# Routed attention and a feed-forward block on one core: group maxima kept in PSUM, one load moved, and a new order of the first batch

## The chip, the cores and the metric

The kernel runs on one core of one Trainium2 chip. The metric is the device time of one execution in microseconds (us); the median of the runs counts. Engines are named as the profile names them: PE (TensorE), DVE (VectorE), ACT (ScalarE), POOL (GpSimd) and SP (the queue from which nearly all transfers are started).

## The reference, cut to what matters

```
q, k, v: 4 batches x 8 heads x 768 tokens x 64;  centroids: 8 heads x 16 x 64
q_assign = argmax(normalised q . normalised centroids)     # same for k
mask     = q_assign[i] == k_assign[j]
attn     = softmax(where(mask, q k^T / 8, -1e9))
x        = (attn v), heads side by side                    # 3072 x 512
h    = x @ w_in                                            # 3072 x 1024
solu = h * softmax(h)
ln   = (solu - mean) / sqrt(var + 1e-6) * g_ln
out  = ln @ w_out                                          # 3072 x 512
```

## The kernel before, in words

**The work.** Heads are taken in pairs, four pairs for each of four batches; a step of batch b, pair p, is called by its kind and b.p. For each pair, queries (i = 0) and keys (i = 1) are loaded (`ld`, L388 for the first batch and the next batch's first pair in two big loads, L419 in eight small ones afterwards), turned so that the 64 channels of two heads lie on partitions, and multiplied by the normalised centroids (`cl`: the cluster products, L469 or L474, into the PSUM tile `csc`). VectorE transposes the products out of PSUM (`tb`, L483), takes the largest of each group of 16 (`mx`, L496), compares each product with its group's largest (`oh`, the one-hot rows, L502 or L508) and transposes these back (`ot`, L518 or L521). The one-hot rows are then copied under the channels of q and k (`pl`, L536 to L551), beside the casts of q and k to bfloat16 (`ca`, L452 to L456). A score matmul over channels and one-hot rows together applies the mask: two tokens of one cluster get 256 more, which the exponential's bias takes off again.

**The first five pairs** (0.0 to 0.3 and 1.0) are "apart": TensorE turns the tokens (`tp`, L400, three transposes each) and VectorE or ACT copies them out of PSUM (`xa`, L407); in later pairs VectorE transposes them itself (`xt`, L425). The very first pair is worked on head by head, in steps with a further index, so that head 0 can start before head 1 has been loaded.

**Attention.** Scores come in banks of 128 keys x 512 (`S`, L637, three PSUM buffers), ACT takes the exponential (`E`, L643, nine SBUF buffers), TensorE multiplies by v with a column of ones (`V`, L660) and VectorE divides (`N`, L672 and L685) into x. v is loaded by `lv` (L563) and cast by `cv` (L568, POOL). In batch 0 the row blocks are ordered so that the first rows of all heads are done early.

**Feed-forward.** For each block of 128 rows x is transposed by a DMA on SP's queue (`tx`, L715), multiplied by w_in (`h`, L746), and VectorE takes the row maximum (`hm`, L752), ACT the exponential (`ex`), VectorE the product (`u`, L765) and its statistics (`bn`, `ag`), SP's queue the transpose of u (`tu`), TensorE the second product (`y`, L810), ACT or VectorE the scaling (`sc`), SP's queue the store (`ou`). The weights are loaded by `li` and `lo`, w_in is cast by `wi` (POOL, L587), g is transposed by `gt` (TensorE, L594), and w_out is centred by `su`, `sk`, `me` and eight steps `ce` (L623, VectorE). The second row block's first matmul (h1.0.0) needs the bank of PSUM from which the last `ce` reads.

**What sets the order.** `Weave.ORDER` (L28 to L84) is a written order for each of the engines SP, POOL, PE, DVE and ACT. A word such as `S2` stands for the next two steps of kind S; `=pl0.0.1.0.0` takes a step by its name. Each engine works strictly through its list; waits between engines follow from the data. Steps that share the PSUM buffer "m" (`cl`, `gt`, `y`) take it and hand it back (`take`, `give`): the cluster products hold it until `tb` has transposed them out (L1030). Before the list begins, the centroids, the first pair's queries and keys and its v are loaded (L841 to L845); `lv0.0` in SP's list is an empty step. `fl` are filler matmuls.

Of the kernel before, what the change touches and what calls it, by code (L numbers as in the profile page):

```python
# [10 lines left out]
F32 = mybir.dt.float32  # L11
# [11 lines left out]
class Weave:  # L23
# [6 lines left out]
        ld4 lv si ld2 lg ld2 lv ld2 lv li lo ld2 lo lv ld2 lo2 ld6 li3 tx lv ld tx ld7 lv tu ld5 lv  # L30
        tx tu ld2 ou ld tu ld10 lv ou tu ld6 tu lv ld lv ld6 ou ld tx ld tu ld3 ou2 ld tx ld3 lv ld
        tu ld tx ld tu ld8 ou ld6 ou ld tu ld3 pl ld3 ou lv tu lv tu ld2 ou ld2 ou tx ld tu tx lv
        ld3 =pl3.2.1.1 pl ou lv2 tx ou tu2 ou pl tu2 tx2 tu ou tx ou tu tx tu ou tx ou tu ou tu ou
        tu ou5
    """
    ORDER["POOL"] = """
        z po zo =ca0.0.0.1.0 cf pl =cv0.0.1 =ca0.0.1.1.1 ca cv =ca0.1.0.1 z =pl0.0.1.0.0
        =pl0.0.1.1.1 pl2 =z5 =ca0.1.1.0 =ca0.1.1.1 ca =ca0.2.0.1 =ca0.2.1.1 pl =pl0.1.0.0 pl2
        =ca0.2.1.0 ca =cv0.1.1 cv =ca0.3.0.1 cv pl =pl0.2.0.0 =pl0.2.0.1 pl gs cv =ca0.3.1.1
        =ca0.3.1.0 ca pl =pl0.3.0.0 sg pl z pl cv ca wi cv =pl1.0.0.1 pl cb pl2 wi =ca1.0.1.0 wi2  # L40
        =ca1.1.1.0 ca2 =cv1.0.1 cv ca =ca1.1.1.1 z at =pl1.1.0.1 pl at pl bl ca al pl =ca1.2.0.1 at
        =cv1.1.1 =ca1.2.1.1 cv =ca1.2.1.0 al ca al =pl1.2.1.1 =ca1.3.1.0 =pl1.2.0.0 pl cv bl pl cv2
        ca2 =pl1.3.1.1 ca pl2 at2 bl al pl =ca2.0.1.1 =ca2.0.1.0 ca =pl2.0.0.1 =pl2.0.1.1 pl2 at
# [143 lines left out]
def kernel(  # L187
# [15 lines left out]
    P = 128  # L203
# [1102 lines left out]
```

## Time and profile before

| what | value |
|---|---|
| median of three runs | 224.43 us (224.42 to 225.3) |
| the profiled execution, its own time | 224.15 us |
| its span from the first to the last instruction | 222.4 us |
| mean moved by the DMA engines | 38.80 MB, 174 GB/s |
| exponentials of the scores (L643) | 288, 150.3 us busy on ACT |
| score matmuls (L637) | 648, 98.4 us busy on PE |
| comparisons of the first five pairs (L502) | 6, 348 to 1717 ns |

The page of the profile gives the busy time of each engine, the chain of work that ended last (followed back from the last instruction to whatever released each step), and the groups of instructions by line. A row of a timeline or of the chain reads: start, duration, engine, line or tile, and how many instructions were merged; in square brackets stands the idle time of the engine just before it and what ended it. A merged row's duration runs from the first start to the last end, so single durations overlap a little with the next one. "To landing" is the time from the issue of a DMA to its completion.

### The profile page before, as it was taken

How to read it: one execution, taken by the hardware profiler on the slowest of the kernel's cores; microseconds unless marked ns; L12 is line 12 of the kernel's file. 1: busy time of each engine (PE TensorE's matmuls, PEld its weight loads, DVE VectorE, ACT ScalarE, POOL GpSimd, SP SyncE). 2: the span in 40 equal slices, each digit the busy share in tenths (PEclk: the TensorE clock that was granted, in tenths of full speed). 3: DMA queues.
4: the chain of work that ended last, by engine and by line, in shares of the span. 5: the costliest groups of instructions: out<-in, count | busy, mean ns of one | idle time of the engine just before them, and what ended most of it. 6: DMA issues, size and time to landing. Idle time of an engine off the chain costs nothing.

```text
span 222.4 us, 6659 instructions
## 1 busy us (share of the span) xinstructions
PE 213.6 (96%) x2437; PEld 144.4 (65%) x2470; DVE 194.9 (88%) x348; ACT 192.4 (87%) x370; POOL 132.9 (60%) x257
## 2 busy tenths in 40 slices
PE   7799999999999999999999999999999999999993
PEld 7587675676666677676567666776675776664442
DVE  2888698899999989988999999898999998889981
ACT  4699898999999999998998998988998999884362
POOL 4589969991684686475968856794448330125231
PEclk9999999999999999999999999999999999999999
DMA  6999998499999999799998969997953415858722
GB/s 197 362 381 352 221 114 266 92 184 175 181 179 144 200 152 235 145 151 211 203 159 156 197 108 255 191 159 169 274 85 84 71 27 124 135 121 115 218 93 96
DMA packets 117327, 38.80 MB, mean 174 GB/s; under 512 B 105640, under 2 KB 112816, under 8 KB 117296
## 3 DMA queue, kind: packets, MB, share of 16 engines
q1 hardware_dynamic: 116864, 37.87, 81.7%
q10 hardware_dynamic: 432, 0.52, 0.7%
q8 instruction: 19, 0.31, 0.6%
q14 instruction: 12, 0.10, 0.2%
HBM read 23.11 MB, written 6.29 MB: 132 GB/s over the span
## 4 chain that ended last, share of the span: by engine, by line
PE 84%; DVE 9%; DMA 2%; issue 1%; ACT 1%; SPq 0%; ACTq 0%; DVEq 0%
PE sps L637 27%; PE hreg L746 17%; PE yps L810 16%; PE ops L660 15%; PE csc L474 4%; PE hreg L400 3%; DMA raw<-in_k_dram 2%; DVE w_out_c L623 2%; DVE x L685 1%; PE csc L469 1%; DVE nmax L752 1%; PE hreg L609 1%; DVE u L765 1%; DVE bs L776 1%; PE hreg L810 1%
## 5 line engine op out<-in xcount | busy, mean ns | idle before, releaser
L643 ACT ACTIVATE e<-sps 128x512 bf16<-128x512 f32 x288 | 150.3, 606 | 10.4 <-PE sps L637 8.5
L637 PE MATMUL sps<-qk 80*128 80x256 bf16 (+3 forms) x648 | 98.4, 260 | 0.3
L637 PEld LDWEIGHTS <-qk 80*128 80x128 bf16 (+1 forms) x648 | 51.6, 97 | 34.0 <-issue 10.2
L660 PEld LDWEIGHTS <-e 128*128 128x128 bf16 x1152 | 52.7, 97 | 11.5 <-PE sps L637 1.1
L660 PE MATMUL ops<-v,e 128*128 128x65 bf16 x1152 | 57.7, 193 | 0.6 <-DVE x L685 0.5
L746 PE MATMUL hreg<-w_in_sb,xT 128*128 128x512 bf16 x175 | 50.4, 379 | 1.2 <-DMA xT<-x 0.2
L810 PE MATMUL yps<-w_out_c,uT 128*128 128x512 bf16 x168 | 46.8, 378 | 0.7
L765 DVE TENSOR_TENSOR u<-e_sb,hreg 128x1024 bf16<-128x1024 bf16 (+1 forms) x25 | 28.9, 1160 | 4.0 <-ACT e_sb L758 3.7
L550 POOL COPY qk<-oht 32x384 f32<-32x384 f32 x40 | 20.3, 507 | 19.3 <-DVE oht L521 14.5
L776 DVE BATCH_NORM_STATS2 bs<-u 128x6 f32<-128x512 bf16 x48 | 31.7, 674 | 0.1
L752 DVE TENSOR_REDUCE nmax<-hreg 128x1 f32<-128x1024 f32 x24 | 29.1, 1213 | 2.5 <-PE hreg L746 2.2
L758 ACT ACTIVATE e_sb<-hreg,nmax 128x1024 bf16<-128x1024 f32 x24 | 26.9, 1119 | 3.3 <-DVE nmax L752 3.2
L792 POOL TENSOR_SCALAR esq<-es,mv 128x1 f32<-128x1 f32 x24 | 8.5, 354 | 33.7 <-DVE mv L780 33.0
L454 POOL CAST qk<-xt 64x768 bf16<-64x768 f32 (+1 forms) x32 | 26.3, 823 | 2.6 <-ACT xt L407 0.8
L456 POOL TENSOR_SCALAR qk<-xt 64x768 bf16<-64x768 f32 (+1 forms) x29 | 24.3, 839 | 2.9 <-PE sps L637 1.2
L810 PEld LDWEIGHTS <-uT 128*128 128x128 bf16 x200 | 17.9, 97 | 10.8 <-issue 0.2
L746 PEld LDWEIGHTS <-xT 128*128 128x128 bf16 x192 | 16.6, 97 | 9.2 <-DVE u L765 1.0
L425 DVE STREAM_TRANSPOSE xt<-raw 128x768 f32<-128x768 f32 x22 | 20.7, 953 | 0.0
L685 DVE TENSOR_TENSOR x<-ops,den 128x256 bf16<-128x256 f32 (+1 forms) x39 | 19.0, 486 | 1.3
L568 POOL CAST v<-vf 128x384 bf16<-128x384 f32 x29 | 14.7, 514 | 3.2 <-PE sps L637 2.3
L825 ACT ACTIVATE y<-yps,alpha 128x512 f32<-128x512 f32 x13 | 8.9, 688 | 7.6 <-PE yps L810 5.8
L795 POOL TENSOR_TENSOR alpha<-esq,halves 128x1 f32<-128x1 f32 x24 | 13.4, 560 | 2.0
(87 smaller groups left out, 178.5 us busy)
## 6 DMA issues: line engine op xcount, KB each, us to landing
vf<-in_v_dram SPq DMA_DIRECT2D x16, 384.0 KB, 4.7
out_dram<-y SPq DMA_DIRECT2D x23, 256.0 KB, 2.7
raw<-in_q_dram SPq DMA_DIRECT2D x44, 96.0 KB, 3.7
raw<-in_k_dram SPq DMA_DIRECT2D x44, 96.0 KB, 3.6
w_st<-in_moe_w_in_dram SPq DMA_DIRECT2D x4, 512.0 KB, 6.7
w_g<-in_moe_w_out_dram SPq DMA_DIRECT2D x4, 512.0 KB, 9.3
raw<-in_q_dram SPq DMA_DIRECT2D x4, 384.0 KB, 7.1
raw<-in_k_dram SPq DMA_DIRECT2D x4, 384.0 KB, 7.5
```

The lines of the kernel that those rows point to most:

```text
L454: VEC[e].tensor_copy(dst, src)
L456: VEC[e].tensor_scalar(dst, src, scalar1=inv_C, scalar2=1.0, op0=Alu.mult, op1=Alu.mult)
L637: nc.tensor.matmul(sps_[n, k][:, c0:c0 + w], side(b, h // 2, 1, h % 2, keys)[r], side(b, h // 2, 0, h % 2, slice(s0 * P, s0 * P + w))[r])
L643: nc.scalar.activation(es[n, k][:, :w], sps_[n, k][:, :w], Act.Exp, scale=exp_scale, bias=-exp_scale)
L660: nc.tensor.matmul(opss[g][:, s, :VW], es[n, k][:, c0:c0 + P], v1[slot(b, h // 2)][:, h % 2, kt, :VW], start=(kt == 0), stop=(kt == n_t - 1))
L685: nc.vector.tensor_tensor(dst, src, dn, op=Alu.mult)
L746: uses(nc.tensor.matmul(hreg[:, at(f, f2)[1], :], xTs[f][:, dc, :], w_in_sb[:, dc, f2 * FF2:(f2 + 1) * FF2], start=(dc == 0), stop=(dc == ...
L752: uses(nc.vector.tensor_reduce(ff[f, "nmax"][:], pair_of(f), axis=AXY, op=Alu.max, negate=True), *both(f))
L758: uses(nc.scalar.activation(ff[f, "e"][:], pair_of(f), Act.Exp, bias=ff[f, "nmax"][:], accum_out=ff[f, "esum"][:]), *both(f))
L765: uses(nc.vector.tensor_tensor(ff[f, "u"][:, at_], ff[f, "e"][:, at_], pair_of(f)[:, at_], op=Alu.mult), *banks)
L776: nc.vector.bn_stats(ff[f, "bs"][:, f2, :], ff[f, "u"][:, f2, :])
L810: ins = nc.tensor.matmul(dst, ff[f, "uT"][:, at(f, f2)[0] * (n_fc // 2) + c, :], w_out_c[:, fc, cols], start=(fc == chunks[0]), stop=(fc = ...
```

## The change

1. **Maxima in PSUM.** For the pairs 0.1, 0.2, 0.3 and 1.0 the tile `csc` is made 24 columns wider, and `mx` writes the group maxima into these columns, where they were written to an SBUF tile before. `oh` reads them from there. The buffer "m" is therefore handed back after `oh` and not after `tb`. The first pair (two half steps) and all later pairs keep the SBUF tile.
2. **The first v.** Its load leaves the place right behind the first pair's queries and keys and becomes the step `lv0.0` of SP's list, behind both loads of pair 0.1 and the queries of pair 0.2.
3. **New orders** for the first batch and the beginning of the second, on all five engines; from `ld2.0.0.0` (SP), `al1` (POOL), `h3.1.0` (PE), `bn2.0` (DVE) and `E29.1` (ACT) on, the lists are as before. Which engine does which step is unchanged. Six of 22 filler matmuls are dropped. Among the moves: on ACT `xa0.0.0.1`, `ca0.0.0.0.0` and `ca0.0.1.1.0` come before `xa0.0.1.1`, `ca0.0.0.1.1` goes in front of the first exponential and `ca0.0.1.0.1` behind the fifth; on PE `tp0.1.0.0` goes in front of `cl0.0.1` and `tp0.1.0.1` in front of the first scores, `cl1.1` goes behind the first feed-forward block (`h0.0.0` to `h0.1.1`), which moves up; on POOL `cv0.0.0` goes behind `ca0.1.0.1` and `ca0.1.1.0`; on DVE `xa0.3.0.1` goes behind N0, `ot0.2` before `xa0.3.1.1`, `xt1.1.1` behind seven centrings, `tb1.1` and `mx1.1` behind the last one; on SP `li0` goes three loads back, `li1` to `li3` and `tx0` come in front of the last two loads of pair 1.1, and `lv1.0` behind most of pair 1.2.

The diff, its orders cut to the lines in question:

```diff
     ORDER["SP"] = """
-        ld4 lv si ld2 lg ld2 lv ld2 lv li lo ld2 lo lv ld2 lo2 ld6 li3 tx lv ld tx ld7 lv tu ld5 lv
+        ld4 si ld3 lv ld lg lv ld2 lv ld lo ld lo ld lo li ld lv lo li ld4 li2 tx ld9 lv ld tx ld tu
+        ld5 lv tu lv ld tx ld tu ou ld10 lv ou tu ld6 tu lv ld lv ld6 ou ld tx ld tu ld3 ou2 ld tx
...
     ORDER["POOL"] = """
-        z po zo =ca0.0.0.1.0 cf pl =cv0.0.1 =ca0.0.1.1.1 ca cv =ca0.1.0.1 z =pl0.0.1.0.0
-        =pl0.0.1.1.1 pl2 =z5 =ca0.1.1.0 =ca0.1.1.1 ca =ca0.2.0.1 =ca0.2.1.1 pl =pl0.1.0.0 pl2
-        =ca0.2.1.0 ca =cv0.1.1 cv =ca0.3.0.1 cv pl =pl0.2.0.0 =pl0.2.0.1 pl gs cv =ca0.3.1.1
-        =ca0.3.1.0 ca pl =pl0.3.0.0 sg pl z pl cv ca wi cv =pl1.0.0.1 pl cb pl2 wi =ca1.0.1.0 wi2
+        z po zo =ca0.0.0.1.0 ca cf pl ca =z4 =z3 =ca0.1.0.1 =ca0.1.1.0 sg cv =pl0.0.1.0.0
+        =pl0.0.1.0.1 =pl0.0.1.1.1 pl cv ca2 =pl0.1.0.0 =ca0.2.1.1 =pl0.1.0.1 pl cv2 pl ca =ca0.2.1.0
+        =pl0.2.0.1 =pl0.2.0.0 ca pl z =ca0.3.1.0 pl =cv0.2.1 ca =ca0.3.1.1 cv pl =pl0.3.0.0 gs ca
+        =cv0.3.1 =pl0.3.0.1 pl cv =pl1.0.1.1 pl3 wi cb wi =ca1.0.0.1 wi2 =ca1.0.1.0 z ca =ca1.1.0.0
...
     ORDER["PE"] = """
-        wm fl2 cp tp fl2 tp ci tp fl4 cl tp fl6 cl fl8 tp S2 tp S tp S tp S V tp V S3 cl S2 tp2 S2 tp S V
-        gt V3 tp S2 tp S cl S2 V tp V S V S tp S V2 S V S2 cl S V S2 tp V S V2 S2 tp S V2 S tp S V S
-        tp V S3 cl S2 V2 S V2 S2 su S V S V S V2 S2 su S2 V2 S2 V2 S2 me S2 V S V2 S2 V S cl S3 V3 S
-        V S h2 S3 h2 S2 V2 S V S V S h2 V S V S h S V2 S2 h S h S V S V S h S V S V S y2 V2 S y S h2
+        wm fl2 cp tp fl2 tp ci tp fl4 cl tp fl8 tp cl tp S3 tp3 S tp S2 cl S tp S2 V tp V2 S2 V gt S V
+        tp2 S2 V cl S V S tp S2 V S tp V S2 tp V S2 V2 S2 cl S V S V S V2 S2 tp S tp S V S V S tp V
+        S2 V S cl S3 V4 S2 su S V S2 V3 S2 su S3 V4 S3 me S V S2 V S V S V S2 V2 S2 h S V S h V S h
+        S h S V S V S V2 S cl S h2 S V S h S V S V S V h S3 V h V S V S V h S y2 S y V S2 h2 S3 y V
...
     ORDER["DVE"] = """
-        cn cg ca tb mx oh ot pl2 tb xa mx xa oh ot =xa0.1.1.1 xa2 tb mx oh xa gk ot xa N tb mx xa oh
-        xa ot N2 tb =xa1.0.0.1 xa mx xa2 N oh ot tb mx N oh ot N sk xt N xt ce2 N ce3 tb ce2 N mx hm
-        ce N u xt bn N hm oh ot bn xt u ag N bn hm sc bn u tb bn N bn mx hm oh =ag2 ag =xt1.3.1 ot u
+        cn cg ca tb mx oh ot pl2 xa tb xa3 mx oh ot xa tb mx oh xa gk ot N tb mx =xa0.3.1.0 xa oh ot
+        xa N tb mx oh N xa =xa1.0.1.0 xa2 ot N tb N mx oh ot N sk N xt ce3 N ce4 xt N hm ce N u bn
+        tb bn mx ag N hm =xt1.2.1 oh u ot bn xt hm sc N u tb bn2 N bn mx hm oh =ag2 ag =xt1.3.1 ot u
...
     ORDER["ACT"] = """
-        wa ct xa2 ca cj =xa0.0.1.1 xa =ca0.0.1.0.1 =ca0.0.1.1.0 pl E5 ca E5 xa E2 xa E xa E56 ex E12
-        ex E7 ex E11 ex sc E8 ex E3 ca E21 ex E17 sc E5 ex E3 sc E4 ex E9 ex E11 ex E5 sc E9 ex E13
+        wa ct xa3 cj ca =ca0.0.1.1.0 xa pl ca E5 ca E3 xa E4 xa2 E56 ex E11 ex E8 ex E12 ex sc E8 ex
+        E3 ca E21 ex E17 sc E5 ex E3 sc E4 ex E9 ex E11 ex E5 sc E9 ex E13 ex E20 ex E5 sc E2 ex E11
...
-        csc = ps_m.tile([P, HALF], F32, name="csc", tag="m")
+        csc = ps_m.tile([P, HALF + HALF // NC_], F32, name="csc", tag="m")
...
-        asg[b, p, hf, "mx"] = pr.tile([P, HALF // NC_], F32, name="mx")
+
+        asg[b, p, hf, "mx"] = (asg[b, p, hf, "csc"][:, HALF:] if apart(b, p) and hf is None else
+                               pr.tile([P, HALF // NC_], F32, name="mx"))
...
             load_head(0, 0, i, hh, nc.sync if i else nc.scalar)
-    load_v(0, 0)
...
-            add(f"lv{t}", "SP", 0.0, -1990, lambda e: None, [], last_ld[-1:], move=1.3)
+            add(f"lv{t}", "SP", 0.45, -990, (lambda e, b=b, p=p: load_v(b, p)), [], last_ld[-1:], move=1.05)
...
                 [f"cl{t}"] + ([f"oh{old}"] if old else []),
-                give="m")
+                give=None if apart(b, p) and not half else "m")
...
                 also={"POOL": 0.7},
+                give="m" if apart(b, p) and not half else None)
...
-                            ("si", "SP", 3.95)):
-        add(name, eng, busy, -1000, lambda e: None, [], ["lv0.0"] if eng == "SP" else [])
+                            ("si", "SP", 3.95)):
+        add(name, eng, busy, -1000, lambda e: None, [], ["ld0.0.1.1"] if eng == "SP" else [])
```

More of the change, by code (lines that the diff above doesn't have):

```diff
@@ new lines @@
+        V S V cl S2 V2 S y S2 y S V S V S V2 S y S2 y S V2 S2 V2 h S2 h2 S h S2 h S V y V2 S V y S
+        V2 y2 S2 h3 S V S2 V cl V h2 S2 V cl S V S V S h S2 h S y S h S V2 y2 S2 y V2 S2 h S V2 S2 h
+        S h2 V2 S V S2 V h y2 V S2 y S V y S2 h S2 V2 cl S V S h S V S2 cl S V2 S h2 S y S V S y V
+        S2 V y2 V h S V S h V S2 cl S2 V S y V y3 S V S V S y S2 V2 S V2 S y S2 y S y V3 S V S2 h2
+        S2 h2 V S V S V S y S V S y S y V S V h y S2 h S h2 S2 V3 S2 V h V cl S h S h S V S2 h S V S
@@ L1029 @@
                 (lambda e, b=b, p=p, hf=hf: turn_back(b, p, hf)),
-                [f"cl{t}"] + ([f"oh{old}"] if old else []), give="m")
+                [f"cl{t}"] + ([f"oh{old}"] if old else []),
+                give=None if apart(b, p) and not half else "m")
             add(f"mx{t}", "DVE", 0.37 if half else 0.56, first - 9,
@@ L1035 @@
                 [f"mx{t}"] + ["zo"] * apart(b, p) + [f"ot{x}" for x in last[-1:]] * (apart(b, p) and not half),
-                also={"POOL": 0.7})
+                also={"POOL": 0.7},
+                give="m" if apart(b, p) and not half else None)
             nd = [f"oh{t}"]
```

32 lines of the change are left out of this document (13 added, 19 removed).

## The prediction

> **What bounds the kernel now.** I read the span and the clock first, then the busy shares and the chain that ended last on the page, then that chain in order of time, then single engines in the stretches where the chain leaves TensorE.
>
> ```profile
> core 0: 222.4 us, clock 1.000
> ```
>
> ```profile
> PE 213.6 (96%) x2437; PEld 144.4 (65%) x2470; DVE 194.9 (88%) x348; ACT 192.4 (87%) x370; POOL 132.9 (60%) x257
> ...
> PE 84%; DVE 9%; DMA 2%; issue 1%; ACT 1%; SPq 0%; ACTq 0%; DVEq 0%
> ```
>
> The clock is full throughout, so nothing here is throttling. TensorE carries 84% of the chain. The change leaves the matmuls themselves alone (it drops six filler matmuls), so what can be won is the 16% in which the chain is elsewhere. It leaves TensorE for long in three places that the edited orders reach:
>
> ```profile
> 1.63 5.31 DMA raw<-in_k_dram
> 6.98 0.56 PE hreg L400 x3
> 7.56 0.86 ACT xt L407 x2
> 8.84 0.52 ACT qk L452
> 9.39 0.52 ACT qk L536
> 10.04 0.60 PE sps L637 x4
> ...
> 23.26 0.53 DVE xt L407
> 23.79 0.88 DVE w_out_c L518
> 24.79 0.57 DVE x L685
> ...
> 43.79 1.97 DVE w_out_c L623 x3
> 45.76 0.49 DVE cst L483
> 46.26 1.29 DVE w_out_c L623 x2
> 48.10 0.46 DVE mx L496
> 48.56 1.23 DVE nmax L752
> 49.79 0.67 DVE w_out_c L623
> 50.50 0.60 PE hreg L746 x2
> ```
>
> Place one, up to 10.04: the first scores (S0.0, head 0 of the first pair) wait for a copy of one-hot rows on ACT (9.39, L536). That copy stands in ACT's queue behind copies and casts of head 1, whose keys land at 1.63 + 5.31 = 6.94. Place two, 23.26 to 25.36: VectorE is late with a copy of turned tokens, a transpose of one-hot rows and the division N1. Place three, 43.79 to 50.46: VectorE works through the centring of w_out (L623) with other work strewn between, and the first matmul of the second feed-forward row block (50.50) waits for its last piece. The written orders of all engines run together again by about 65 us, so from there I take over the shift that has been reached.
>
> **The change, part by part.**
>
> *The start.* In the new ACT order only one copy of head 1 (xa0.0.1.1) stands between the landing and the one-hot copy: it ends at 7.56 + 0.43 (half of 0.86) = 7.99. The one-hot copy then waits for the transposed one-hot rows instead, which VectorE has ready when its own two copies of them begin:
>
> ```profile
> 8.58 0.57 DVE L536 COPY qk<-oht 16x192 f32<-16x192 f32 x2
> ...
> 21.61 1.72 DVE L502 TENSOR_TENSOR w_out_c<-cst,mx 128x384 bf16<-128x384 f32 x1
> ...
> 31.30 0.55 DVE L502 TENSOR_TENSOR w_out_c<-cst,mx 128x384 bf16<-128x384 f32 x1
> ...
> 43.15 0.18 DVE L672 RECIPROCAL den<-ops 128x4 f32<-128x4 f32 x1 [0.55 <-PE ops L660]
> ```
>
> VectorE's copies end at 9.15, ACT's at 8.58 + 0.52 = 9.10. TensorE now has three steps in front of S0.0: transposes of the second pair's queries (tp0.1.0.0), head 1's cluster products, more transposes (tp0.1.0.1).
>
> ```profile
> 8.47 0.53 PE L469 MATMUL csc<-xt,w_out_c 128*32 128x192 f32 x8 [0.62 <-ACT xt L407]
> ```
>
> The first needs its data. Today those queries are the second load behind head 1's keys (v is the first):
>
> ```profile
> 2.58 0.47 SPq L388 DMA_DIRECT2D raw<-in_q_dram  x1
> ```
>
> ```profile
> raw<-in_q_dram SPq DMA_DIRECT2D x1, 384.0 KB, 6.4
> ```
>
> They land at 2.58 + 6.4 = 8.98, which is 2.04 behind the keys, so 1.02 for each load of 384 KB. Without v they take the first slot, 7.96. Then the transposes end near 8.5 (0.56 for three), the products near 9.05, the second transposes near 9.4 when pipelined and at 9.6 when not. S0.0 starts near 9.35 instead of 10.04. ACT's cast ca0.0.0.1.1 moves in front of the first exponential (0.52 from 9.10 on) and fits beside S0.0; ca0.0.1.0.1 takes its old place behind the fifth. **Gain at the start 0.7 us**, between 0.4 (10.04 less 9.6) and 0.9 (less 9.15).
>
> *v three loads later* lands in the fourth slot, 6.94 + 4 x 1.02 = 11.0. Its cast on POOL now stands behind two casts of the second pair, the later of which needs VectorE's fourth copy of turned tokens: 9.15 + 4 x 0.53 + 0.49 (a transpose between) = 11.8. A cast of this size takes
>
> ```profile
> 18.15 0.83 POOL L456 TENSOR_SCALAR qk<-xt 64x768 bf16<-64x768 f32 x1
> ```
>
> so POOL reaches v near 12.6, 1.6 us after it has landed. Behind v on POOL are four one-hot copies that head 1's scores need. At no more than ACT's 0.52 for each of the five, they end by 15.2. The exponentials get to head 1 after nine of 0.52 (8.77 / 17, below), a cast and a copy: 9.8 + 4.7 + 0.95 = 15.4. Price nothing; past that cover each microsecond falls on ACT, one to one.
>
> *The maxima in PSUM.* For four pairs the maximum is written beside the products, and the comparison (L502) reads one operand from SBUF and one from PSUM. The same comparison took 1.72 at 21.61 and 0.55 at 31.30. I take 0.55 for all, the nearer row: 1.17 us less in VectorE's queue ahead of N1. The other end is that the 1.72 stays; no row shows a PSUM operand dearer, the division at 24.79 reads PSUM and takes 0.57. By the Trainium skill, SBUF — State Buffer, section Who interferes with whom, a VectorE operation with two SBUF inputs contends with a GpSimd operation that reads SBUF, and one with a single SBUF input does not; the trace agrees in that 0.55 and 1.72 are the same instruction on the same shapes. Another of its rules speaks against the change: Perfetto Trace Analysis, section Optimizing Scalar/DVE Operations, puts the overhead of a VectorE instruction at about 125 ns on PSUM and 60 on SBUF. By that, as an estimate, the eight edited instructions would cost 0.5 us more and the total gain would be 1.1 us; the row of 24.79 shows nothing of it.
>
> The price: the PSUM buffer comes free after the comparison, later by a maximum and a comparison (0.46 + 0.55 = 1.0). Next in it is the transpose of g on TensorE, behind that the scores S3.2 and all that follow; ACT waits for these. Three banks of scores in hand last 3 x 0.52 = 1.5 us, so I price it at nothing, at most 1.0 if they are used up.
>
> *Place two.* ACT shows what it costs:
>
> ```profile
> 25.10 0.60 ACT L643 ACTIVATE e<-sps 128x512 bf16<-128x512 f32 x1 [0.58 <-PE sps L637]
> 26.16 8.77 ACT L643 ACTIVATE e<-sps 128x512 bf16<-128x512 f32 x17 [0.46 <-PE sps L637]
> ```
>
> Behind it 17 exponentials run without a gap, so ACT's loss of 0.58 + 0.46 = 1.04 is real. N1 comes earlier by 1.17 (the comparison) and 0.7 (the start), near 22.9, and the copy that cluster products cl0.3 need stays in front of it. **Gain 1.0**, between 0 and 1.04. Sum so far 1.7.
>
> *Place three* is a queue of VectorE. The new order takes a transpose out of PSUM (0.49) and a maximum (0.46) from in front of the last centring. It puts a transpose of tokens (xt1.1.1; 0.9, like the one at 23.79) in, which so far stood ahead of all centrings. One centring (0.66, a third of 1.97) goes into the idle 0.55 at 43.15. Net gain 0.6, so the last centring ends 2.3 earlier, near 48.2. But the 0.95 comes back right behind it, on an engine that is 88% busy: 1.4 for VectorE at 65 us, 1.7 for TensorE. **I carry 1.6 on**, with 0.7 and 2.3 as ends.
>
> *SP's queue.* The last two of the eight loads for the second batch's second pair now stand behind the first transposing DMA of x (tx0), which waits for the division N6:
>
> ```profile
> 40.33 1.86 SPq L715 DMA_TRANSPOSE xT<-x  x1
> 42.30 0.52 SPq L563 DMA_DIRECT2D vf<-in_v_dram  x1
> 42.91 0.61 SPq L419 DMA_DIRECT2D raw<-in_q_dram  x1
> ```
>
> ```profile
> raw<-in_q_dram SPq DMA_DIRECT2D x1, 96.0 KB, 3.9
> ```
>
> With 1.7 gained it starts near 38.6 and ends near 40.5; the last load is issued 0.6 later and lands 3.9 after that, at 45.0. VectorE's xt1.1.1 wants it at 47.55 (where the sixth and seventh centrings end) less 1.7, 0.49 and 0.55: 44.8. Price 0.2, inside my rounding. The first feed-forward matmul is moved up too, closer behind the casts of its weights on POOL; 0 to 0.83, one cast, taken as 0.
>
> **Sum.** 0.7 + 1.0 = 1.7; place three's 0.6 is more than paid back by the 0.95 on VectorE, which leaves 1.4 there and 1.7 on TensorE: 1.6 us. The profiled execution took 224.15 (span 222.4); it becomes 222.55. The median of the runs shown is 0.28 above it, so 222.8 stands for the median. About 0.5%, 1.12 us, is what a measurement of this kernel can tell from no change: faster means below 223.3, slower above 225.55.
>
> **The rivals.**
>
> *Only the start is kept.* Place two comes back at another wait, or the comparison stays at 1.72. For it: TensorE is 96%, VectorE 88% and ACT 87% busy, so an engine that is freed soon meets another. Against: 17 exponentials in a row show no other stall of ACT for 9 us. Gain 0.7, time 223.7: same.
>
> *The last key load comes late.* The transpose xt1.1.1 waits, and behind it in VectorE's queue a division, the maximum of the first row block and the last centring; TensorE waits at the matmul of 50.50. Each microsecond beyond a landing of 3.9 counts one to one, and the 0.95 behind it can't be caught up. With VectorE's 1.4 it decides from a landing of 5.3 us; at 7.0, a little over the 6.4 that a load took in the full queue of the start, the kernel is 1.7 slower: 226.1. For it: a transposing DMA is right ahead in the queue. Against: the load issued at 42.91 had one ahead as well, and took 3.9.
>
> *More is won.* VectorE's idle time behind 50 us absorbs the 0.95, and 2.3 stays, or 2.5 with the start at its better end: near 222.0.
>
> **How the numbers follow.** Forecast 0.48, more won 0.10: faster, 0.58. Only the start 0.27: same. The late load 0.15: slower. The range takes in the better end with what lies between runs (221.4), the start-only case, and the late load up to a landing of 6 us, which is 0.7 slower (225.1). The forecast's own range is 222.2 to 223.5.
>
> **What would show it.** Right: first scores near 9.4; four comparisons near 0.55; no idle of ACT near 0.5 between 20 and 27; the gapless run of exponentials that began at 26.16 beginning near 24.5; the last centring ending near 48.2. Wrong: a comparison over 0.8; VectorE idle in front of xt1.1.1 with the load of keys as releaser; TensorE idle in front of the first L746.

## The result, and the profile after

The kernel after takes 226.2 us (median of 22 runs, 224.05 to 229.79), the kernel before took 224.43 us beside it (22 runs, 223.64 to 226.34). The ratio is 1.0056, 95% interval 1.0036 to 1.0075: slower by 1.3 us, where 1.6 us faster had been forecast. The ratio leaves out the runs that took over 1.5% more than the fastest of their kernel, four of the 22 of the kernel after, so it lies below the ratio of the two medians. The profiled execution took 226.73 us.

The page of the kernel after: span, busy time of each engine, shares of the chain that ended last.

```profile
span 224.9 us, 6673 instructions
...
PE 216.9 (96%) x2464; PEld 144.7 (64%) x2464; DVE 194.2 (86%) x348; ACT 192.6 (86%) x370; POOL 132.3 (59%) x257
...
PE 80%; DVE 9%; DMA 5%; ACT 2%; issue 2%; POOL 1%; ACTq 0%; DVEq 0%; POOLq 0%
```

TensorE's share of the chain fell from 84% to 80%, and transfers rose from 2% to 5%. The engines are as busy as before; more of the chain now runs through DMAs. (Line numbers from the products on are two higher than before.)

ACT's timeline of the kernel after: start, duration, what was done, and in brackets the idle time ahead.

```profile
10.27 2.85 ACT L645 ACTIVATE e<-sps 128x512 bf16<-128x512 f32 x5
...
19.51 5.50 ACT L645 ACTIVATE e<-sps 128x512 bf16<-128x512 f32 x11 [0.15 <-PE sps L639]
25.47 5.99 ACT L645 ACTIVATE e<-sps 128x512 bf16<-128x512 f32 x12 [0.47 <-PE sps L639]
31.62 2.55 ACT L645 ACTIVATE e<-sps 128x512 bf16<-128x512 f32 x5 [0.16 <-PE sps L639]
...
69.80 1.11 ACT L760 ACTIVATE e_sb<-hreg,nmax 128x1024 bf16<-128x1024 f32 x1
```

The same in the kernel before:

```profile
10.46 2.56 ACT L643 ACTIVATE e<-sps 128x512 bf16<-128x512 f32 x5 [0.56 <-PE sps L637]
...
20.18 4.33 ACT L643 ACTIVATE e<-sps 128x512 bf16<-128x512 f32 x8 [0.15 <-PE sps L637]
...
69.31 1.11 ACT L758 ACTIVATE e_sb<-hreg,nmax 128x1024 bf16<-128x1024 f32 x1
```

The first exponential comes at 10.27 (10.46 before). From there to the 42nd exponential of the scores ACT is idle for 0.15 + 0.47 + 0.16 us, where it was for 0.15 + 0.58 + 0.46 before (the last two in front of the rows at 25.10 and 26.16). The last row of each is the exponential of the fourth feed-forward row block: it stands at 69.80 now and stood at 69.31 before, so the gain of the first 50 us is gone by then.

VectorE's timeline of the kernel after: comparisons, one maximum written to PSUM, the moved transpose of tokens, the last centring.

```profile
15.42 0.55 DVE L504 TENSOR_TENSOR w_out_c<-cst,csc 128x384 bf16<-128x384 f32 x1
...
19.80 0.56 DVE L498 TENSOR_REDUCE csc<-cst 128x24 f32<-128x384 f32 x1
...
21.24 0.54 DVE L504 TENSOR_TENSOR w_out_c<-cst,csc 128x384 bf16<-128x384 f32 x1
...
26.05 0.56 DVE L504 TENSOR_TENSOR w_out_c<-cst,csc 128x384 bf16<-128x384 f32 x1
...
33.87 0.56 DVE L504 TENSOR_TENSOR w_out_c<-cst,csc 128x384 bf16<-128x384 f32 x1
...
45.77 0.98 DVE L425 STREAM_TRANSPOSE xt<-raw 128x768 f32<-128x768 f32 x1
...
48.45 0.74 DVE L625 SCALAR_TENSOR_TENSOR w_out_c<-w_g,g_ln,hreg 128x512 bf16<-128x512 f32 x1
```

The last centring in the kernel before:

```profile
49.70 0.74 DVE L623 SCALAR_TENSOR_TENSOR w_out_c<-w_g,g_ln,hreg 128x512 bf16<-128x512 f32 x1
```

The comparisons of the four pairs take 0.54 to 0.56. The transpose at 45.77 has no bracket: it did not wait for its keys. The last centring starts 1.25 earlier than before.

SP's queue in the kernel after (start, time on the queue):

```profile
39.26 1.35 SPq L717 DMA_TRANSPOSE xT<-x  x1
40.65 2.46 SPq L419 DMA_DIRECT2D raw<-in_k_dram  x2
43.22 2.72 SPq L419 DMA_DIRECT2D raw<-in_q_dram  x4
46.03 2.01 SPq L419 DMA_DIRECT2D raw<-in_k_dram  x3
48.14 0.60 SPq L565 DMA_DIRECT2D vf<-in_v_dram  x1
48.79 0.58 SPq L419 DMA_DIRECT2D raw<-in_k_dram  x1
49.48 1.88 SPq L717 DMA_TRANSPOSE xT<-x  x1
```

The second transposing DMA of x in the kernel before:

```profile
43.82 1.39 SPq L715 DMA_TRANSPOSE xT<-x  x1
```

TensorE in the kernel after, from the first scores on, where its idle time ahead is over 0.25:

```profile
9.85 0.81 PE L639 MATMUL sps<-qk 80*128 80x256 bf16 x6 [0.35 <-DVE qk L538]
...
55.49 0.61 PE L748 MATMUL hreg<-w_in_sb,xT 128*128 128x512 bf16 x2 [1.06 <-DMA xT<-x]
...
99.86 0.61 PE L748 MATMUL hreg<-w_in_sb,xT 128*128 128x512 bf16 x2 [1.28 <-DMA xT<-x]
```

The first scores (10.04 before) wait for VectorE's copy of one-hot rows. The second transposing DMA is issued 5.7 us later than before, and TensorE waits 1.06 us for it. At 99.86 it waits 1.28 for a later one. Neither of these two waits was in the forecast.

### The profile page after: what moved, and what is told of

Read it like the earlier page. It is cut to its first block, busy times and chain, and to the rows that moved or that the text cites. A ratio compares the mean times of both kernels' runs of the same rounds, so it can differ in the third digit from the quotient of the medians.

```text
span 224.9 us, 6673 instructions
## 1 busy us (share of the span) xinstructions
PE 216.9 (96%) x2464; PEld 144.7 (64%) x2464; DVE 194.2 (86%) x348; ACT 192.6 (86%) x370; POOL 132.3 (59%) x257
## 4 chain that ended last, share of the span: by engine, by line
PE 80%; DVE 9%; DMA 5%; ACT 2%; issue 2%; POOL 1%; ACTq 0%; DVEq 0%; POOLq 0%
PE sps L639 24%; PE hreg L748 17%; PE yps L812 15%; PE ops L662 13%; DMA xT<-x 5%; PE csc L474 4%; PE hreg L400 2%; ACT e L645 2%; PE csc L469 1%; PE idle_p L855 1%; DVE xt L407 1%; PE hreg L611 1%; DVE u L767 1%; DVE oh L510 1%; DVE bs L778 1%
## 5 line engine op out<-in xcount | busy, mean ns | idle before, releaser
L662 PE MATMUL ops<-v,e 128*128 128x65 bf16 x1152 | 58.4, 193 | 0.0
L748 PE MATMUL hreg<-w_in_sb,xT 128*128 128x512 bf16 x192 | 54.3, 379 | 2.3 <-DMA xT<-x 2.3
L812 PE MATMUL yps<-w_out_c,uT 128*128 128x512 bf16 x184 | 50.0, 378 | 0.0
L456 POOL TENSOR_SCALAR qk<-xt 64x768 bf16<-64x768 f32 (+1 forms) x29 | 24.5, 845 | 3.2 <-PE sps L639 1.1
L788 POOL TENSOR_SCALAR es<-esum 128x1 f32<-128x1 f32 x24 | 5.4, 230 | 15.9 <-ACT e_sb L760 15.5
```

Of the source, the lines that this page charges most:

```text
L456: VEC[e].tensor_scalar(dst, src, scalar1=inv_C, scalar2=1.0, op0=Alu.mult, op1=Alu.mult)
L662: nc.tensor.matmul(opss[g][:, s, :VW], es[n, k][:, c0:c0 + P], v1[slot(b, h // 2)][:, h % 2, kt, :VW], start=(kt == 0), stop=(kt == n_t - 1))
L748: uses(nc.tensor.matmul(hreg[:, at(f, f2)[1], :], xTs[f][:, dc, :], w_in_sb[:, dc, f2 * FF2:(f2 + 1) * FF2], start=(dc == 0), stop=(dc == ...
L812: ins = nc.tensor.matmul(dst, ff[f, "uT"][:, at(f, f2)[0] * (n_fc // 2) + c, :], w_out_c[:, fc, cols], start=(fc == chunks[0]), stop=(fc = ...
```

## The experiments

Theory 1 was that the late second transposing DMA costs the time; rival 2, that the new orders of the compute engines do; rival 3, that transposing DMAs are just in time everywhere, so that a lead is lost at the next one. A fourth theory came out of the runs. In SP's list, the head is what stands up to the first transposing DMA of x and the last load of pair 1.1, and the tail is the rest. Each kernel is compared with the kernel before on the same chip.

**One part of the change at a time**

*The second transposing DMA put back.*

```diff
-        ld4 si ld3 lv ld lg lv ld2 lv ld lo ld lo ld lo li ld lv lo li ld4 li2 tx ld9 lv ld tx ld tu
+        ld4 si ld3 lv ld lg lv ld2 lv ld lo ld lo ld lo li ld lv lo li ld4 li2 tx ld2 tx ld7 lv ld2 tu
```

> The kernel after, with the second transposing DMA of x put back on SP's queue ahead of pair 1.2's loads (right behind the last load of pair 1.1). Theory 1 (the loss between 55 and 62 us is the late transposing DMA: issued at 49.48 in the kernel after, 43.82 before): it is issued near 43.5, the wait of TensorE on it (1.06 us at 55.49) is gone, the row maxima of the tile at 62.04 start near 60.5, and about 1.5 us of it last to the end if the later transposing DMAs keep their distance: 0.993 to 0.997 of the time before. Rival 2 (the new orders of TensorE, VectorE and GpSimd cost it, whatever SP does): the wait goes, the time stays at 1.004 to 1.007. Rival 3 (all transposing DMAs are just in time, whoever is early waits at the next): 60.5 is reached, but the wait for the transposing DMA at 94 us takes 1 to 1.5 us more, and the time is 0.999 to 1.003.

Measured 224.69 us, ratio 1.0024 (0.9998 to 1.0051). The DMA was issued at 42.80 and its wait was gone: about 0.3% came back, with intervals that overlap, and less than theory 1 asked for; the ratio lies where rival 3 put it. The next late transfer stepped in, the v load that the cast on GpSimd needs (TensorE waited 0.28 for that cast at 54.09):

```profile
53.53 0.50 POOL L570 CAST v<-vf 128x384 bf16<-128x384 f32 x1 [3.80 <-DMA vf<-in_v_dram]
```

*SP's old order from the second batch on, all else new.*

```diff
-        ld4 si ld3 lv ld lg lv ld2 lv ld lo ld lo ld lo li ld lv lo li ld4 li2 tx ld9 lv ld tx ld tu
-        ld5 lv tu lv ld tx ld tu ou ld10 lv ou tu ld6 tu lv ld lv ld6 ou ld tx ld tu ld3 ou2 ld tx
+        ld4 si ld3 lv ld lg lv ld2 lv li lo ld2 lo lv ld2 lo2 ld6 li3 tx lv ld tx ld7 lv tu ld5 lv
+        tx tu ld2 ou ld tu ld10 lv ou tu ld6 tu lv ld lv ld6 ou ld tx ld tu ld3 ou2 ld tx
```

> The kernel after, with SP's order of the kernel before from the first loads of the second batch on (the first v load stays fourth; the compute engines keep the new orders). Theory 1: all transposing DMAs go out as early as before (43.8, 58.0, 92.9 us), so neither wait of 1.0 to 1.3 us on them comes back; the loads of pair 1.1 come in the old order, which the new compute order may wait for by up to 0.5; 0.993 to 0.998 of the time before. Rival 2: 1.003 to 1.007, as the new compute orders are all still there. Rival 3: 0.998 to 1.003, with the wait near 94 us above 1 us.

Measured 224.06 us, ratio 0.9978 (0.9954 to 1.0002). Against the kernel after's 1.0056 that is 0.8%, 1.7 us, for SP's order alone. Rival 2 falls: the new compute orders are all still in it. The profile's lead of 1.17 us at the fourth row block shrinks to 0.32 at the last, in part at a transposing DMA as rival 3 has it:

```profile
97.53 0.38 PE L748 MATMUL hreg<-w_in_sb,xT 128*128 128x512 bf16 x1 [0.67 <-DMA xT<-x]
```

*The maxima alone, put into the kernel before.*

```diff
-        csc = ps_m.tile([P, HALF], F32, name="csc", tag="m")
+        csc = ps_m.tile([P, HALF + HALF // NC_], F32, name="csc", tag="m")
...
-                [f"cl{t}"] + ([f"oh{old}"] if old else []), give="m")
+                [f"cl{t}"] + ([f"oh{old}"] if old else []),
+                give=None if apart(b, p) and not half else "m")
```

(with the lines of the change's diff for `mx` and `oh`)

> The kernel before, with nothing but the maxima of the four large pairs kept in the PSUM tile of the products (the tile given back by the comparison); all orders are the old ones, the first v load is in its old place. The three dear comparisons cost 0.55 instead of 0.89, 1.72 and 0.85: 1.8 us less on VectorE. All theories: the first batch's centring ends up to 1 us earlier. If the place where a gain is carried to the end is TensorE's order and not VectorE's, this moves the time by less than 0.5 us: 0.997 to 1.000. If VectorE's time at the start is what the first exponentials wait for, 0.995 to 0.997. If the products' tile, held longer, delays the next products, above 1.001.

Measured 224.02 us, ratio 0.9987 (0.9969 to 1.0004): nothing that can be told from no change. In the profile the saving comes back as another wait. The comparisons take 0.54 to 0.55, and of the two waits of ACT at place two (0.58 and 0.46) one of 0.15 is left. Then the cluster products of pair 1.0 wait on TensorE for the comparison of pair 0.3, which hands back the PSUM buffer, and ACT idles 0.87 at 32.66 in its turn:

```profile
31.39 0.85 PE L469 MATMUL csc<-xt,w_out_c 128*32 128x384 f32 x8 [0.72 <-DVE w_out_c L503]
```

So in the old orders the buffer that is held longer has a price. The kernel after, with the new orders, has no such wait.

*The kernel after without the maxima in PSUM* (the same lines taken back).

> The kernel after, with the maxima back in SBUF and the tile given back by the turning copy, as before; all orders are the new ones. Theory 1 (the maxima are worth what the comparisons save, about 1.2 us ahead of the second pair's centring, and that is carried up to 55 us and lost at the late transposing DMA): the milestone at 55.34 comes near 56.5, the wait on the transposing DMA shrinks to about 0, and the time stays within 0.3% of the kernel after, 1.003 to 1.008. If the gain of the maxima is carried to the end after all: 0.5 to 1.2 us slower than the kernel after, 1.008 to 1.011.

Measured 225.18 us, ratio 1.0049 (1.0025 to 1.0072), as the kernel after within the intervals. Its comparisons, now with two operands in SBUF again:

```profile
14.77 0.56 DVE L503 TENSOR_TENSOR w_out_c<-cst,mx 128x384 bf16<-128x384 f32 x1
20.60 0.72 DVE L503 TENSOR_TENSOR w_out_c<-cst,mx 128x384 bf16<-128x384 f32 x1
25.40 0.88 DVE L503 TENSOR_TENSOR w_out_c<-cst,mx 128x384 bf16<-128x384 f32 x1
33.23 0.56 DVE L503 TENSOR_TENSOR w_out_c<-cst,mx 128x384 bf16<-128x384 f32 x1
```

The 1.72 of the kernel before is gone by the order alone; PSUM saves 0.5 us in sum (2.7 against 2.2), where the old orders' 4.0 promised 1.8. The expectation failed in two more points: the milestone (the exponential of the second row block) came at 54.55 and not at 56.5, and TensorE still waited 1.15 us for the second transposing DMA.

*The same in the kernel with the old loads.*

> The kernel of e2_old_loads with the maxima back in SBUF. By e4_no_psum the four comparisons then cost 0.56, 0.72, 0.88 and 0.56 us in the new orders: 0.5 us more on VectorE, where the old orders had 0.89, 1.72, 0.55 and 0.85. If the maxima in PSUM are worth nothing at the end, the time is that of e2_old_loads, 0.996 to 1.000 of the time before; if the 0.5 us lie on the path, 0.999 to 1.002.

Measured 223.86 us, ratio 0.9980 (0.9957 to 1.0003). Three times over, the maxima are worth nothing at the end that can be told from noise.

*The v load alone, in the kernel before.*

```diff
-        ld4 lv si ld2 lg ld2 lv ld2 lv li lo ld2 lo lv ld2 lo2 ld6 li3 tx lv ld tx ld7 lv tu ld5 lv
+        ld4 si ld3 lv ld lg lv ld2 lv li lo ld2 lo lv ld2 lo2 ld6 li3 tx lv ld tx ld7 lv tu ld5 lv
```

> The kernel before with nothing but the first v load put behind three more loads of queries and keys. The prediction's term for the start: the first exponential 0.4 to 0.9 us earlier than in kernels with the old place (10.46 and 11.02 us in two profiles, which themselves lie 0.56 apart), so near 10.0. If that is carried to the end, 0.996 to 0.998; if a later wait takes it (v is cast later, or the transposing DMAs near 44 and 98 us don't come earlier), 0.999 to 1.001.

Measured 224.49 us, ratio 1.0007 (0.9988 to 1.0027); first exponential at 10.42. Nothing that can be told from noise reaches the end.

*SP's new order alone, in the kernel before* (its list taken whole, the v load with it).

> The kernel before with the whole new order of SP's queue and of the first v load, all compute orders and the maxima as before: the second transposing DMA of x goes behind eight more transfers. Theory 1 (the late transposing DMA is the loss, whoever computes): issued near 50 and landing at 54 to 56, where TensorE wants it at 54.6: a wait of up to 1.3 us there, 1.000 to 1.006 of the time before. Rival 2 (the new compute orders cost it): 0.997 to 1.000, and no wait for that DMA.

Measured 230.41 us, ratio 1.0261 (1.0225 to 1.0296): more than four times the loss of the kernel after, which no theory had. VectorE and SP's queue:

```profile
45.79 0.98 DVE L425 STREAM_TRANSPOSE xt<-raw 128x768 f32<-128x768 f32 x1 [5.36 <-POOL w_in_sb L587]
```

```profile
40.46 1.55 SPq L715 DMA_TRANSPOSE xT<-x  x1
42.06 1.31 SPq L419 DMA_DIRECT2D raw<-in_k_dram  x2
```

The old order of VectorE wants the second keys of pair 1.1 ahead of all centrings, and the new order of SP issues their last two loads at 42.06, behind the transposing DMA. The row names a cast on GpSimd that ended at 45.67; the second of the two loads, issued near 42.7, lands near 45.8 if it takes the 3.1 us that such loads took there (the median from 40 to 48), so I read the load as what ended the wait. By this reading the new place of that transpose, behind seven centrings, is what makes the new loads bearable.

**Where rival 3 leads**

*The transposing DMA near 92 us issued earlier.* The kernel with the old loads, and:

```diff
-        tx tu ld2 ou ld tu ld10 lv ou tu ld6 tu lv ld lv ld6 ou ld tx ld tu ld3 ou2 ld tx
+        tx tu ld2 ou ld tu ld10 lv ou tu ld6 tu lv ld lv ld3 tx ld3 ou ld2 tu ld3 ou2 ld tx
```

> The kernel of e2_old_loads (the kernel after with the old order of SP's loads from the second batch on) with the seventh transposing DMA of x, the one near 92 us, issued three loads of keys, one store and one load earlier. Theory 3 (the lead of 1.2 us that e2_old_loads shows at 88 us is lost at the transposing DMAs, first at this one: TensorE waits 0.67 us for it at 97.5): issued near 88.5, the wait of TensorE is gone, the row maxima of 101.67 start near 101.1, and 0.4 to 0.7 us more reach the end: 0.994 to 0.997 of the time before. Rival (the loads that now come behind it are as late, and the wait moves to the transposes of queries and keys near 107 us): the wait at 97.5 goes, the time stays at 0.997 to 0.999.

Measured 227.26 us, ratio 1.0122 (1.0096 to 1.0149). I had taken the wrong division for its operand. SP's queue and VectorE:

```profile
84.39 2.25 SPq L416 DMA_DIRECT2D raw<-in_q_dram  x3
92.50 1.25 SPq L717 DMA_TRANSPOSE xT<-x  x1
```

```profile
104.45 0.98 DVE L425 STREAM_TRANSPOSE xt<-raw 128x768 f32<-128x768 f32 x1 [1.79 <-DMA raw<-in_q_dram]
110.94 0.98 DVE L425 STREAM_TRANSPOSE xt<-raw 128x768 f32<-128x768 f32 x1 [1.99 <-DMA raw<-in_k_dram]
```

SP stood still for 5.86 us ahead of it (86.64 to 92.50), and the loads behind came too late. Here a DMA placed ahead of its data held up all that stood behind it: 1.4% or 3.2 us against the kernel with the old loads.

*The product that needs it put later on TensorE* (in the kernel without PSUM and with the old loads).

```diff
-        V S V cl S2 V2 S y S2 y S V S V S V2 S y S2 y S V2 S2 V2 h S2 h2 S h S2 h S V y V2 S V y S
+        V S V cl S2 V2 S y S2 y S V S V S V2 S y S2 y S V2 S2 V2 S2 h3 S h S2 h S V y V2 S V y S
```

> The kernel of e6_old_loads_no_psum with the hidden product that first uses the transposing DMA of 92 us put behind two more score products on TensorE, 0.6 us later in the order. Theory 3 (in the kernels that are ahead, the lead is lost in part where TensorE waits 0.2 to 1.3 us for that DMA, more in one run than in another): the wait is filled, 0.995 to 0.998 of the time before, with a narrower spread. If the loss at 98 us is given back later anyway, as in e2_old_loads at 107 us: 0.997 to 1.000.

Measured 224.65 us, ratio 0.9986 (0.9957 to 1.0014), runs from 222.59 to 227.1: no gain, no narrower spread. Neither attempt to win something where rival 3 points has succeeded; it is not shown, and not ruled out.

**Which part of SP's order**

*The v load and the second transposing DMA early; the v load alone early.*

```diff
-        ld4 si ld3 lv ld lg lv ld2 lv ld lo ld lo ld lo li ld lv lo li ld4 li2 tx ld9 lv ld tx ld tu
+        ld4 si ld3 lv ld lg lv ld2 lv ld lo ld lo ld lo li ld lv lo li ld4 li2 tx lv ld2 tx ld9 tu
```

and `li2 tx lv ld10 tx ld tu` for the second.

> The kernel after with two transfers put back ahead of the seven or more loads of pair 1.2: the first v load of the second batch's group (lv1.0, right behind the first transposing DMA of x) and the second transposing DMA of x (right behind pair 1.1's last load). In e1_tx2_early, whose TensorE ran line by line as in e2_old_loads up to 53 us, the products with v then waited 0.4 us for the cast of that v load, which GpSimd could begin 3.8 us late. Theory 1 in its sharper form (both transfers behind pair 1.2's loads are the loss): no wait on either at 53 to 56 us, and 0.996 to 1.000 of the time before, as e2_old_loads. If the loss is elsewhere in the load order (pair 1.1's loads, or the fourth batch of transposes at 61 us): 1.001 to 1.005, as e1_tx2_early.

> The kernel after with lv1.0 alone put back ahead of pair 1.2's loads; the second transposing DMA of x stays late. Theory 1: it is issued near 49.5 and lands near 55, TensorE waits 1 to 1.5 us for it as in the kernel after, and the time is that of the kernel after, 1.004 to 1.008. If the v load is the whole loss: 0.996 to 1.001.

Measured 225.6 us, ratio 1.0038 (1.0007 to 1.0068), and 225.77 us, 1.0062 (1.0037 to 1.0087). The two differ by 0.2% for the transposing DMA, which is inside their intervals. For the v load these runs are spoilt: ahead of pair 1.1's last two loads it held these back, VectorE waited for the keys, and TensorE waited at 47.7 in the first (at 48.9 in the second). VectorE and TensorE in the first:

```profile
46.10 0.98 DVE L425 STREAM_TRANSPOSE xt<-raw 128x768 f32<-128x768 f32 x1 [1.23 <-DMA raw<-in_k_dram]
```

```profile
47.66 0.35 PE L662 MATMUL ops<-v,e 128*128 128x65 bf16 x6 [1.14 <-DVE x L687]
```

*Only these two transfers late, in the kernel before.*

```diff
-        ld4 lv si ld2 lg ld2 lv ld2 lv li lo ld2 lo lv ld2 lo2 ld6 li3 tx lv ld tx ld7 lv tu ld5 lv
+        ld4 lv si ld2 lg ld2 lv ld2 lv li lo ld2 lo lv ld2 lo2 ld6 li3 tx ld7 lv ld tx lv tu ld5 lv
```

> The kernel before, all its compute orders and its loads of pair 1.1 kept; only lv1.0 and the second transposing DMA of x are moved behind the loads of pair 1.2 on SP's queue, as in the kernel after. Theory 1: issued near 50, landing near 55 where TensorE wants it at 54.6, the cast of v as late as 52 to 53: 0.4 to 1.5 us slower, 1.002 to 1.007. If the two transfers cost something only beside the new compute orders: 0.999 to 1.001. The 2.6 per cent of e8_new_loads_alone then belong to pair 1.1's loads, for which VectorE waited 5.4 us there.

Measured 224.54 us, ratio 1.0015 (0.9987 to 1.0042). The DMA went out at 48.22 and was not waited for. By this run late transfers alone, with the old compute orders, are not the loss, though its interval leaves room for up to 0.4%.

*Both right behind pair 1.1's loads:* `li2 tx ld2 tx lv ld9 tu`. *SP's new head with the old tail:* `li2 tx ld2 lv ld tx ld7 lv tu`, then `ld5 lv tx tu ld2 ou ld tu ld10`. *The old head with the new tail:* `lv li lo ld2 lo lv ld2 lo2 ld6 li3 tx ld7 lv ld tx ld tu`, the rest as after.

> The kernel after with the second transposing DMA of x and lv1.0, in this order, right behind the last load of pair 1.1 and ahead of pair 1.2's loads. Theory 1: no wait of TensorE for x or v between 47 and 58 us, 0.4 to 0.6 us less than e1_tx2_early, whose products waited 0.42 us for the cast of that v load: 0.998 to 1.001 of the time before. If the rest of the loss is not the v load, it stays at 1.001 to 1.005.

> The kernel after with the new order of SP up to the first transposing DMA of x and the last load of pair 1.1, and the old order from there on. If the loss lies in the tail (transposing DMAs and v loads behind loads), the time is that of e2_old_loads, 0.996 to 1.000; if it lies in the head (the last two key loads of pair 1.1 held behind that DMA, the weights), it stays near 1.002 to 1.006.

> The kernel after with the old order of SP up to the first transposing DMA of x (all of pair 1.1's loads ahead of it) and the new order behind it. If the loss lies in the tail: that of the kernel after, 1.003 to 1.007, with a wait of TensorE of about 1 us for the second transposing DMA near 55 us. If it lies in the head: 0.997 to 1.001.

Measured 225.19 us, ratio 1.0017 (0.9988 to 1.0046); 224.84 us, 1.0024 (0.9998 to 1.0051); 223.93 us, 0.9980 (0.9954 to 1.0005). Theory 1 falls here: the old head heals the kernel with the second transposing DMA still late (issued at 47.77), and the new head hurts with the old tail. With the new head TensorE waited for a transpose of u instead:

```profile
57.32 1.04 PE L812 MATMUL yps<-w_out_c,uT 128*128 128x512 bf16 x4 [1.34 <-DMA uT<-u]
```

Its DMA was issued at 53.10. In the kernel with the old loads:

```profile
50.64 1.28 SPq L772 DMA_TRANSPOSE uT<-u  x1
```

Theory 4: the two key loads behind the first transposing DMA push back the whole queue, and whichever transfer is just in time there is waited for.

*Only these two loads moved: ahead of that DMA in the kernel after, behind it in the kernel with the old loads.*

```diff
-        ld4 si ld3 lv ld lg lv ld2 lv ld lo ld lo ld lo li ld lv lo li ld4 li2 tx ld9 lv ld tx ld tu
+        ld4 si ld3 lv ld lg lv ld2 lv ld lo ld lo ld lo li ld lv lo li ld4 li2 ld2 tx ld7 lv ld tx ld tu
```

```diff
-        ld4 si ld3 lv ld lg lv ld2 lv li lo ld2 lo lv ld2 lo2 ld6 li3 tx lv ld tx ld7 lv tu ld5 lv
+        ld4 si ld3 lv ld lg lv ld2 lv li lo ld2 lo lv ld2 lo2 ld4 li3 tx ld2 lv ld tx ld7 lv tu ld5 lv
```

> The kernel after with one move: the last two key loads of pair 1.1 go ahead of the first transposing DMA of x, the rest of SP's new order is kept, the late second transposing DMA included. Theory 4 (the two loads, issued after that DMA, delay the whole queue behind it by 1.3 us or more, and whatever comes just in time there makes TensorE wait): the second transposing DMA is issued near 47.8, as in e15_old_head_new_tail, and not at 49.5; no wait of TensorE near 55 us; 0.996 to 1.000 of the time before. If the loss is in the weights' and the other loads' order: 1.003 to 1.007.

> The kernel of e2_old_loads with the same move the other way: the last two key loads of pair 1.1 behind the first transposing DMA of x. Theory 4: the transposes behind it go out 1.3 to 2.5 us later, TensorE waits for the transpose of u near 57 us as in e14_new_head_old_tail (1.34 us there), and the time is 1.001 to 1.005 of the time before. If the weights' order is the loss: 0.996 to 0.999.

Measured 224.41 us, ratio 1.0011 (0.9989 to 1.0033), and 225.21 us, 1.0037 (1.0009 to 1.0065). Put ahead of the DMA in the kernel after, the two loads give back 0.45% (1.0 us); put behind it in the kernel with the old loads, they cost 0.6% (1.3 us). In both cases the intervals of the two kernels do not overlap. The first is a little above its forecast of 0.996 to 1.000. SP's queue in the first:

```profile
33.46 1.29 SPq L419 DMA_DIRECT2D raw<-in_k_dram  x2
39.69 1.34 SPq L717 DMA_TRANSPOSE xT<-x  x1
...
48.24 1.97 SPq L717 DMA_TRANSPOSE xT<-x  x1
```

SP's queue and TensorE in the second:

```profile
40.40 2.01 SPq L419 DMA_DIRECT2D raw<-in_k_dram  x2
...
51.41 1.27 SPq L772 DMA_TRANSPOSE uT<-u  x1
```

```profile
56.46 1.04 PE L812 MATMUL yps<-w_out_c,uT 128*128 128x512 bf16 x4 [0.37 <-DMA uT<-u]
```

This profile is of the second kernel's shortest run (224.06 us, against a median of 225.21), so its wait of 0.37, where 1.34 was expected, can't account for the whole 1.3 us. What the profiles agree in is which kernels wait: TensorE or its weight loads wait 0.2 to 1.3 us for that transpose of u, at 56.5 to 57.3, in e1, e13, e14 and e17, whose two loads stand behind the DMA, and not in e2, e15 and e16, where they stand ahead (the kernel after and e4 wait for the transpose of x instead, e9 and e10 for the keys).

Ahead of the DMA the two loads cost nothing, since SP only waits there (34.75 to 39.69 in the first). Behind it they take 1.3 to 2.5 us of a queue that is then full. By the Trainium skill, DMA: Bandwidth & Descriptors, section Anatomy of one DMA (which treats DMAs from GpSimd), a wait on a semaphore is made by the sequencer that issues, before dispatch; the trace of SP's queue agrees, as the same two loads went out at 33.46 ahead of the DMA and at 40.65 behind it.

**The stretches side by side.** One profile each: the first exponential of the scores, and the distances from there to the feed-forward exponentials of row blocks 1, 4 and 24.

| kernel | first | to 1 | 1 to 4 | 4 to 24 | ratio |
|---|---|---|---|---|---|
| before | 10.46 | 39.49 | 19.36 | 144.18 | 1 |
| after | 10.27 | 38.29 | 21.24 | 146.12 | 1.0056 |
| second transpose early (e1) | 9.96 | 38.18 | 20.55 | 144.63 | 1.0024 |
| no PSUM (e4) | 9.63 | 38.16 | 21.07 | 144.75 | 1.0049 |
| both behind keys (e13) | 10.62 | 38.18 | 20.50 | 145.29 | 1.0017 |
| new head, old tail (e14) | 9.66 | 38.31 | 21.58 | 144.45 | 1.0024 |
| keys put behind (e17) | 9.99 | 38.17 | 20.53 | 144.56 | 1.0037 |
| transpose and v early (e9) | 9.43 | 39.40 | 20.06 | 144.82 | 1.0038 |
| v early (e10) | 10.73 | 39.39 | 20.06 | 144.80 | 1.0062 |
| old loads (e2) | 10.00 | 38.16 | 19.98 | 145.03 | 0.9978 |
| old loads, no PSUM (e6) | 9.86 | 38.37 | 19.98 | 144.01 | 0.9980 |
| old head, new tail (e15) | 10.39 | 38.24 | 19.98 | 145.25 | 0.9980 |
| keys put ahead (e16) | 10.69 | 38.16 | 19.98 | 144.60 | 1.0011 |

ACT's new list has one exponential less (about 0.5 us) in the first stretch and one more in the second. So the new compute orders win some 0.7 us up to row block 1 and keep it where the second stretch takes 19.98. With the two loads ahead of the DMA it takes 19.98 in every kernel. With them behind it takes 20.50 to 21.58, but for e9 and e10: these take 20.06, after the wait for the keys has cost them 1.2 us in the stretch before.

The last stretch can be narrowed down. From the ninth row block to the 24th all 19 profiles take 98.3 to 98.7 us, and from the fourth to the sixth 20.4 to 21.1; from the sixth to the ninth it is 25.2 to 28.7: 25.40 before, 27.40 in the kernel after, where the wait of TensorE at 99.86 falls and one of VectorE for keys:

```profile
110.62 0.98 DVE L425 STREAM_TRANSPOSE xt<-raw 128x768 f32<-128x768 f32 x1 [0.82 <-DMA raw<-in_k_dram]
```

## Why the prediction was wrong

- **SP's queue** is the step that failed. It followed the two loads behind the first transposing DMA to their own consumer, found a landing at 45.0 and priced 0.2. That part held: the transpose at 45.77 did not wait. It held by little, as VectorE waited 1.2 us there once a v load stood ahead of these keys (e9, e10). What stood behind the two loads on the queue, the second transposing DMA, a v load and the transpose of u, was never priced. Their place costs 1.0 to 1.3 us (e16, e17). All of SP's new order from the second batch on costs 1.7 us (e2); its tail alone, behind the old head, costs nothing that can be told (e15).
- **"From there I take over the shift"** failed too. In the profile of the kernel after 1.94 us more were lost behind the fourth row block, between the sixth and the ninth; in the others of the table the last stretch took 144.0 to 145.3. This loss was not tied to any edit. Even with the old loads, where 1.1 to 1.2 us were ahead at the fourth row block, the medians end only 0.5 us ahead.
- **The start**: 0.7 forecast (0.4 to 0.9), 0.19 in the two profiles shown. The first scores came right behind VectorE's one-hot copies, as forecast, but head 0's cluster products, on which these hang, started at 6.70 in this profile and at 6.10 in that of the kernel before. Over all profiles the first exponential came at 9.43 to 10.73, mean 10.08, in the 14 kernels with the new compute orders, and at 10.46 to 11.02, mean 10.70, in the three with the v load second: 0.6 (10.17 and 10.42 in e8 and e7, which move v but keep the old compute orders). The size agrees with that, and two single profiles can't show it.
- **v three loads later**: priced at nothing, and ACT shows no wait for it.
- **The maxima**: 0.55 us each was right. The saving was taken from the old order, where one comparison took 1.72; in the new orders SBUF costs 0.56 to 0.88. The Trainium skill's rule on two SBUF inputs (SBUF — State Buffer, Who interferes with whom) fits both: beside the comparison of 1.72, at 21.61, GpSimd was casting (21.31 to 22.91), and beside that of 0.55, at 31.30, it stood still from 31.32 on. Its dearer VectorE access to PSUM (Perfetto Trace Analysis, Optimizing Scalar/DVE Operations) is not seen: the maximum at 19.80 took 0.56 into PSUM, and 0.55 into SBUF before. The price of holding the PSUM buffer, put at nothing, is nothing in the new orders and 0.7 us on TensorE in the old ones (e3).
- **Place two**: 1.0 forecast, 0.4 measured (1.19 idle up to the 42nd exponential became 0.78). One wait of 0.47 remained at 25.47, and the exponentials behind it began there and not near 24.5. **Place three**: the last centring 2.3 earlier forecast, 1.25 measured. Together with the start, the lead at row block 4 was 1.1 to 1.2 us in e2 and e6, where 1.6 was forecast: too large, right in sign.
- **The rival of the late key load** gave 226.1, close to the result, but by another mechanism: VectorE was to wait for the keys, and did not. That its number fits is luck.

Open: why e16 (1.0011) and e15 (0.9980) differ, whose intervals overlap; what decides, in a single run, the stretch from the sixth to the ninth row block; and how much of the loss is time on the queue and how much a slower landing. The first three transposing DMAs of x landed 3.2 to 4.2 us after their issue before and in e2, 4.8 to 6.5 in the kernel after, and still 4.1 to 6.2 in e15 and e16. The best kernels, e2, e6 and e15 (0.9978 to 0.9980), are faster than the kernel after; each one's interval reaches just past 1, so none is shown faster than the kernel before by itself.

## What to carry to other kernels

When a transfer is moved on an in-order queue, price all that stands behind it, not its own consumer alone: here two loads ahead of a waiting DMA rode in the wait for free, and behind it they delayed what followed. A written compute order and a written load order can depend on each other (SP's new order cost 2.6% with the old compute orders and 0.8% with the new ones), so test each with the other's old form. And a saving read from one slow row is worth only what that row would still cost in the new order.

## What was not expected of the hardware

In the kernel after a load of 96 KB held SP's queue for about 0.65 us when the queue ran freely (2.72 for four at 43.22) and for 1.2 in one row (2.46 for two at 40.65); a transposing DMA held it for 1.3 to 1.9 in the rows shown. The start of the first exponential varies by 1.3 us between profiles of kernels that share the compute orders of the start. A DMA that waited 5.9 us at the front of SP's queue (e5) made the kernel 1.4% slower than the same kernel without that move.
